# First stage of the second batch on sums and differences of x, two matmuls a piece in place of four

## The chip, the cores and the metric

One core of one Trainium2 chip runs the kernel. The metric is device time in microseconds, the median of several runs. TensorE is called PE here, with PEld for its weight loads, VectorE is DVE, ScalarE is ACT, GpSimd is POOL, SyncE is SP; SPq, ACTq and DVEq are their sequencers.

## The reference

For x of 8 batches, 3008 positions and 256 channels: a real FFT along the positions, a complex 256x256 projection with bias, a soft threshold at 0.01, the inverse FFT, and then a two-layer MLP on all 24064 tokens.

```python
X = np.fft.rfft(x, axis=1)
Yr = Xr @ w_r - Xi @ w_i + b_r
Yi = Xr @ w_i + Xi @ w_r + b_i
Yr = np.sign(Yr) * np.maximum(np.abs(Yr) - lam, 0.0)      # Yi likewise
y = np.fft.irfft(Yr + 1j * Yi, n=x.shape[1], axis=1)
h = y.reshape(B * S, D) @ w_in                            # 256 -> 2048
out = np.maximum(0.01 * h, h) @ w_out                     # 2048 -> 256
```

## The kernel before

The length 3008 is split as 47 x 64, and the transform is done as two stages of matmuls with constant matrices (`fa` for the factor 47, `fb` for 64), the projection between them and two inverse stages (`gb`, `ga`).

`fwd(b)` (L218) is the first stage of batch b. It loads x in seven pieces (L224, the DMA issues at L237 and L240), six of 120x512 and one, number 6, of 120x256. Each piece has two halves xa and xb (`xin`), on which the symmetry of the transform can be used: one half of the output is fa0 applied to the sum xa + xb, the other is fa1 applied to the difference xa − xb. In batch 0 and in batches 2 to 7 `fold` (L242) forms the sum and the difference on VectorE (L247, L248), and `stage_a` (L260) does one product of each. Batch 1 has its own function, `stage_a1` (L273), which works on xa and xb as loaded: fa0·xa + fa0·xb and fa1·xa + (−fa1)·xb, so four matmuls a piece, each of which shows as two records on PE. The negated matrix is the third slice of `fa32`, made by ACT in the set-up. ACT copies the two results over xa and xb (L282) and SP stores them to `u_dram` (L283). The pieces come in the order 0, 1, 2, 3, 6, 4, 5; 4 and 5 use the two banks `psf`, the others the four banks `psh`. The loads of batch 1 may not be issued before a certain read of batch 0 (`reads[-1]`), and its matmuls not before the last but one `stage_g` of batch 0 (`turning[NPAIR - 2]`).

`mid(b)` (L314) is the middle of batch b, in twelve pairs of frequencies: load u (L331), `stage_b` (L336, matmul L345, copy `ef` L349, sum L350), `proj` (L364, through `products`, whose matmuls are all at L80; bias sum `kb` L382, t L390, threshold c L391 and t L392, copies and signs `zf` L396 and L400), and `stage_g` (L412), which stores v to `v_dram` (L418, L420).

`v_load` (L455, DMA issue L461) and `inverse` (L470) turn one pair of columns back into tokens: matmuls with `ga` (L482), the copy `odd` (L485), sum and difference `y` (L486, L488), copies into `yc` (L495). `forms` (L498) makes of a chunk of 512 tokens the hi and lo parts that the MLP multiplies (`yh` L507, `yl` L508). The MLP (`moe_a`, `moe_b`, `moe_o`, the matmuls at L94 and L609) runs over 47 chunks.

`convert_win` (L159) and `load_wout` (L177) make hi and lo parts of the MLP's weights; most of that is on VectorE (L135 to L139, L164, L167 to L174, L203, L204). Two of its tiles, `cva` and `cvq`, take the buffers that are otherwise `vin`'s and `gf`'s.

Batch 0 is done first, ahead of the MLP. Three places are spoken of below. The batch-0 stage is the middle of batch 0, from about 42 to 100 us. The ramp, from 100 to about 120 us, holds the first five pieces of batch 1, the first two pairs of inverses and the end of the weight conversion. Behind it the MLP runs, and pieces 4 and 5 of batch 1 and the work of all later batches are mixed into it. A scheduler sets the order on each engine from the program and its own view of time; each engine takes its instructions in the order it is given, and waits by semaphores.

Of the kernel before, what the change touches and what calls it, by code (L numbers as in the profile page):

```python
# [8 lines left out]
F32 = mybir.dt.float32  # L9
# [11 lines left out]
P = 128  # L21
PA = NK1 * NG
# [8 lines left out]
def spectral_mlp_kernel(  # L31
# [18 lines left out]
    D = w_r.shape[0]  # L50
# [15 lines left out]
    sb = ctx.enter_context(tc.tile_pool(name="sb", bufs=2))  # L66
    dram = ctx.enter_context(tc.tile_pool(name="dram", bufs=2, space=bass.MemoryType.DRAM))
    ps = ctx.enter_context(tc.tile_pool(name="ps", bufs=1, space=bass.MemoryType.PSUM))
    sync, act, dve, pool = nc.sync, nc.scalar, nc.vector, nc.gpsimd

    def bank(tag, bufs):
        return ps.tile([P, 512], F32, name=tag, tag=tag, bufs=bufs)

    def products(dst, pairs):

        terms = []
        for l, r in pairs:
            terms += [(l[0], r[0]), (l[0], r[1]), (l[1], r[0])] if len(l) == 2 else [(l[0], r[0])]
        for i, (a, b) in enumerate(terms):
            last = nc.tensor.matmul(dst, a, b, start=(i == 0), stop=(i == len(terms) - 1))  # L80
        return last
# [14 lines left out]
    def flat(t):  # L96
        return t.rearrange("p a b -> p (a b)")


    consts = {}  # L100
# [117 lines left out]
    def fwd(b):  # L218
        ud = dram.tile([2, NK1, NG * NS, D], F32, name="u_dram", tag="u_dram", bufs=NPRE + 1)
        u_dram[b] = ud  # L220
        uv = ud.rearrange("c k (g s) d -> c (k g) (s d)", g=NG)
        x_t, s_t = {}, {}

        def load(c):  # L224
            cols = slice(2 * c * D, min(2 * c + 2, NS) * D)
            n = cols.stop - cols.start
            if b < NPRE:
                tag, bufs = (XT, XT1)[b][c]
                x2 = sb.tile([PA, 2, 2 * D], F32, name="xin", tag=tag, bufs=bufs)
                x_t[c] = [x2[:, h, :n] for h in range(2)]  # L230
            else:
                x_t[c] = [
                    sb.tile([PA, 2 * D], F32, name=f"xin{h}", tag="uv"[h], bufs=3 - h)[:, :n] for h in range(2)
                ]
            for h, t in enumerate(x_t[c]):
                if b == 0:
                    (act if h else sync).dma_start(t, x[b, h, :, cols])  # L237
                else:
                    with tc.issue_after(reads[-1].ins):
                        sync.dma_start(t, x[b, h, :, cols])  # L240

        def fold(c):  # L242
            xa, xb = x_t[c]
            n = xa.shape[1]
            eng = dve
            xs = sb.tile([PA, 2 * D], F32, name="xs", tag="zf", bufs=1)[:, :n] if b else xs3[:, c % 3, :n]
            eng.tensor_add(xs, xa, xb)  # L247
            eng.tensor_sub(xa, xa, xb)  # L248
            s_t[c] = [(xs,), (xa,)] if b < NPRE else [xs, xa]

        def split(c, h):
            t = s_t[c][h]
            n = t.shape[1]
            z = sb.tile([PA, 2, 2 * D], F32R, name="xz", tag="ez"[h], bufs=1)
            xh, xl = z[:, 0, :n], z[:, 1, :n]
            dve.tensor_copy(xh, t)
            dve.tensor_sub(xl, t, xh.bitcast(F32))  # L257
            s_t[c][h] = (xh, xl)

        def stage_a(c, h):  # L260
            t = x_t[c][h]
            n = t.shape[1]
            pa = (bank("psf", 2) if b else bank("psh", 4))[:PA, :n]
            products(pa, [(consts[f"fa{h}"] if b else consts[f"fa{h}32"], s_t[c][h])])
            t = x_t[c][1 - h]
            cp = act.copy(t, pa)
            if b == 0:
                turned[:] = [cp]
            st = (act if b else sync).dma_start(uv[h, :, 2 * c * D:2 * c * D + n], t)
            if b == 0:  # L270
                written.append(st)

        def stage_a1(c):  # L273

            n = x_t[c][0].shape[1]
            pas = [(bank("psf", 2) if c in (4, 5) else bank("psh", 4))[:PA, :n] for _ in range(2)]
            for h in range(2):
                with tc.issue_after(turning[NPAIR - 2].ins):
                    products(pas[h], [
                        (consts[f"fa{h}32"], (x_t[c][0],)), (consts[f"fa{2 * h}32"], (x_t[c][1],))])  # L280
            for h in range(2):
                act.copy(x_t[c][h], pas[h])  # L282
                sync.dma_start(uv[h, :, 2 * c * D:2 * c * D + n], x_t[c][h])  # L283

        if b == 1:
            for c in range(NX):
                load(c)
                yield 0
            for c in (0, 1, 2, 3, 6, 4, 5):
                stage_a1(c)  # L290
                yield 6 * x_t[c][0].shape[1]
            return

        ahead = 2 if b >= NPRE else NX
        for c in range(ahead):
            load(c)
        yield 4 * CS if b >= NPRE else 0
        fold(0)
        if b >= NPRE:
            split(0, 0)  # L300
        yield 0
        for c in range(NX):
            for h in range(2):
                if h == 0 and c + ahead < NX:
                    load(c + ahead)
                if h == 0 and c + 1 < NX:
                    fold(c + 1)
                stage_a(c, h)
                if b >= NPRE and (c + h < NX):
                    split(c + h, 1 - h)  # L310
                yield 3 * x_t[c][h].shape[1]


    def mid(b):  # L314
# [49 lines left out]
        def proj(j):  # L364

            e = e_t.pop(j)
            ps_k = bank("psf", 2) if b else bank("pso", 2)
            ps_y = None if b else bank("psf", 2)
            for dst, c, w in ((0, 2, "wr"), (0, 1, "wn"), (D, 0, "wd")):
                if c == 1 and b:  # L370
                    ps_y = bank("psf", 2)
                with tc.issue_after(mlp[0].ins) if b and c == 2 else nullcontext():
                    products((ps_k if c == 2 else ps_y)[:, dst:dst + D], [
                        (tuple(t[:, a, c, :] for t in e), tuple(t[:, a, :] for t in consts[w]) if b else (consts[w + "32"][0][:, a, :],)) for a in range(NH)
                    ])
                if c == 2:
                    kc = ps_k[:, :D]
                    if b:
                        kc = sb.tile([P, D], F32, name="kc", tag="kc")
                        act.copy(kc, ps_k[:, :D])  # L380
                    kb = sb.tile([P, 2, D], F32, name="kb", tag="kb", bufs=1)
                    (pool if b else dve).tensor_add(kb, bias, kc.unsqueeze(1).broadcast_to([P, 2, D]))  # L382
                if c:
                    yield 6 * D
                if c == 2 and b and j:
                    stage_g(j - 1)
                    yield 3 * CS
            t = sb.tile([P, 2, D], F32, name="t", tag="t" if b else "v", bufs=1 if b else 2)
            c = sb.tile([P, 2, D], F32, name="c", tag="kb" if b else "yt", bufs=1)
            dve.tensor_add(flat(t), ps_y, flat(kb))  # L390
            dve.tensor_scalar(c, t, LAMBDA, -LAMBDA, ALU.min, ALU.max)  # L391
            thresholded.append(dve.tensor_sub(t, t, c))  # L392
            zf = z0[j % 3] if b == 0 else sb.tile([P, 2, D], F32, name="zf", tag="zf", bufs=1)
            for i in range(2):
                s = slice(64 * i, 64 * (i + 1))
                act.copy(zf[:64, i, :], t[s, 0, :])  # L396
                if b == 0 and j == NPAIR - 1:
                    dve.tensor_scalar(zf[64:, i, :], t[s, 1, :], sign[s, NK1 + j:NK1 + j + 1], None, ALU.mult)
                else:
                    act.mul(zf[64:, i, :], t[s, 1, :], sign[s, NK1 + j:NK1 + j + 1])  # L400
            if b == 0:
                z_t[j] = (zf,)
                yield 6 * D
                return
            z = sb.tile([P, 2, 2, D], F32R, name="zh", tag="z", bufs=1)
            zh, zl = z[:, 0], z[:, 1]
            act.copy(zh, zf)
            dve.tensor_sub(zl, zf, zh.bitcast(F32))
            z_t[j] = (zh, zl)
            yield 6 * D  # L410
# [273 lines left out]
    FWD = NS * 6 * D  # L684


    fa32 = sb.tile([PA, 3, PA], F32, name="fa32", tag="xi", bufs=1)
    for h in range(2):
        sync.dma_start(fa32[:, h], fa[h])
    for h in range(3):  # L690
        consts[f"fa{h}32"] = (fa32[:, h],)
    xs3 = sb.tile([PA, 3, 2 * D], F32, name="xs3", tag="yl")
    f0 = Stream(fwd(0), FWD)
# [10 lines left out]
    win_tmp = (  # L704
        sb.tile([P, NH * NIN], F32, name="cva", tag="vin"), sb.tile([P, NH * NIN], F32, name="cvq", tag="gf"),
        sb.tile([P, 4, 2, P], F32, name="ws", tag="yh"))
    act.mul(fa32[:, 2], fa32[:, 1], -1.0)
    convert_win(0)
    with tc.issue_after(turned[0].ins):
        split_consts()  # L710
# [162 lines left out]
```

## Time and profile before

| | us |
|---|---|
| median of 3 runs | 2574.14 |
| lowest and highest | 2566.14, 2575.76 |
| the profiled execution | 2568.88 |
| its span on the core | 2567.1 |

The mean granted clock of PE in the profiled execution is 0.995 of full speed. The rows below are of that one execution: busy times by engine, stretches of time with the busy time of each engine, single instructions with their start and duration, and what ended a wait. A count behind an x is a number of instructions that stand together on one engine.

### The profile page before, as it was taken

How to read it: one execution, taken by the hardware profiler on the slowest of the kernel's cores; microseconds unless marked ns; L12 is line 12 of the kernel's file. 1: busy time of each engine (PE TensorE's matmuls, PEld its weight loads, DVE VectorE, ACT ScalarE, POOL GpSimd, SP SyncE). 2: the span in 40 equal slices, each digit the busy share in tenths (PEclk: the TensorE clock that was granted, in tenths of full speed). 3: DMA queues.
4: the chain of work that ended last, by engine and by line, in shares of the span. 5: the costliest groups of instructions: out<-in, count | busy, mean ns of one | idle time of the engine just before them, and what ended most of it. 6: DMA issues, size and time to landing. Idle time of an engine off the chain costs nothing.

```text
span 2567.1 us, 42449 instructions
## 1 busy us (share of the span) xinstructions
PE 2527.2 (98%) x16204; PEld 2269.8 (88%) x16204; DVE 1882.8 (73%) x3460; ACT 1677.5 (65%) x3151; POOL 118.9 (5%) x96
## 2 busy tenths in 40 slices
PE   6999999999999999999999999999999999999999
PEld 4689888999899998999989999899998998999998
DVE  7787777777877778777787677867768777666665
ACT  4776666677566765677666676567665676655564
POOL 0001000000000000000000000000000000000000
PEclk8999999999999999999999999999999999999999
DMA  8631133111321113111141111412114111100000
GB/s 267 176 93 50 42 91 88 41 50 45 103 67 46 50 37 112 59 49 49 42 113 53 50 49 38 120 54 58 34 38 132 46 54 41 44 21 29 9 17 17
DMA packets 119904, 165.12 MB, mean 64 GB/s; under 512 B 13597, under 2 KB 69909, under 8 KB 119701
## 3 DMA queue, kind: packets, MB, share of 16 engines
q1 hardware_dynamic: 79112, 115.54, 14.7%
q10 hardware_dynamic: 40589, 46.87, 7.1%
q8 instruction: 128, 2.10, 0.4%
q14 instruction: 75, 0.61, 0.1%
HBM read 86.60 MB, written 75.76 MB: 63 GB/s over the span
## 4 chain that ended last, share of the span: by engine, by line
PE 89%; DMA 4%; DVE 3%; ACT 2%; issue 1%; ACTq 0%; SPq 0%; DVEq 0%
PE pso L609 38%; PE psh L94 34%; PE psf L80 11%; PE psf L482 3%; PE psf L345 3%; DMA xin<-x_dram 1%; DMA u_dram<-xin 1%; PE psh L80 1%; DVE gl L562 1%; DMA v_dram<-v 0%; DMA u<-u_dram 0%; DVE xz L257 0%; DVE gf L593 0%; ACT zf L400 0%; DMA vin<-v_dram 0%
## 5 line engine op out<-in xcount | busy, mean ns | idle before, releaser
L94 PE MATMUL psh<-yh,win_hi 128*128 128x256 f32 (+1 forms) x2608 | 741.3, 285 | 2.1 <-DVE gf L593 2.0
L94 PE MATMUL psh<-yl,win_hi 128*128 128x256 f32 (+1 forms) x2608 | 732.3, 281 | 0.0
L94 PE MATMUL psh<-yh,win_lo 128*128 128x256 f32 (+1 forms) x2608 | 729.6, 281 | 0.0
L562 DVE TENSOR_TENSOR gl<-gf,gh 128x1024 fp32r<-128x1024 f32 x376 | 461.0, 1226 | 309.8 <-ACT gh L560 305.9
L609 PE MATMUL pso<-gl,wout_hi 128*128 128x512 f32 x1504 | 591.6, 393 | 1.1 <-DVE gl L562 1.1
L609 PE MATMUL pso<-gh,wout_hi 128*128 128x512 f32 x1504 | 591.1, 393 | 1.0 <-ACT gh L560 1.0
L609 PE MATMUL pso<-gh,wout_lo 128*128 128x512 f32 x1504 | 589.6, 392 | 0.0
L94 PEld LDWEIGHTS psh<-yh,win_hi 128*128 128x128 f32 x2608 | 489.9, 188 | 19.7 <-DVE gf L593 4.9
L94 PEld LDWEIGHTS psh<-yl,win_hi 128*128 128x128 f32 x2608 | 490.4, 188 | 17.4 <-issue 0.5
L94 PEld LDWEIGHTS psh<-yh,win_lo 128*128 128x128 f32 x2608 | 489.0, 188 | 2.1
L560 ACT CAST gh<-gf 128x1024 fp32r<-128x1024 f32 x376 | 395.3, 1051 | 44.4 <-PE pso L609 34.9
L596 ACT ACTIVATE gf<-gf 128x768 f32<-128x768 f32 x368 | 311.7, 847 | 150.4 <-DVE gf L593 139.4
L609 PEld LDWEIGHTS pso<-gl,wout_hi 128*128 128x128 f32 x1504 | 282.5, 188 | 61.4 <-DVE gl L562 2.9
L609 PEld LDWEIGHTS pso<-gh,wout_hi 128*128 128x128 f32 x1504 | 282.8, 188 | 47.3 <-ACT gh L560 1.8
L609 PEld LDWEIGHTS pso<-gh,wout_lo 128*128 128x128 f32 x1504 | 282.5, 188 | 46.5 <-issue 0.2
L595 ACT ACTIVATE gf<-psh 128x256 f32<-128x256 f32 x368 | 142.0, 386 | 239.1 <-PE psh L94 232.0
L593 DVE TENSOR_TENSOR gf<-psh,u 128x512 f32<-128x512 f32 x368 | 252.4, 686 | 34.4 <-PE psh L94 30.7
L577 ACT COPY p<-psh 128x256 f32<-128x256 f32 x368 | 137.0, 372 | 158.0 <-PE psh L94 149.6
L382 POOL TENSOR_TENSOR kb<-bias,kc 128x512 f32<-128x512 f32 x84 | 116.3, 1385 | 2074.3 <-ACT kc L380 1877.0
L578 DVE TENSOR_TENSOR u<-psh,p 128x256 f32<-128x256 f32 x368 | 154.6, 420 | 73.8 <-ACT p L577 72.6
L580 DVE TENSOR_TENSOR gf<-psh,u 128x256 f32<-128x256 f32 x368 | 154.8, 421 | 31.1 <-PE psh L94 17.2
L581 DVE TENSOR_TENSOR gf<-psh,gf 128x256 f32<-128x256 f32 x368 | 154.5, 420 | 5.5
(128 smaller groups left out, 3173.0 us busy)
## 6 DMA issues: line engine op xcount, KB each, us to landing
u<-u_dram SPq DMA_DIRECT2D x192, 128.0 KB, 2.8
v_dram<-v ACTq DMA_DIRECT2D x192, 128.0 KB, 2.4
out_dram<-ob SPq DMA_DIRECT2D x94, 256.0 KB, 2.0
vin<-v_dram SPq DMA_DIRECT2D x96, 240.0 KB, 3.6
xin<-x_dram SPq DMA_DIRECT2D x90, 240.0 KB, 3.0
u_dram<-xin ACTq DMA_DIRECT2D x72, 240.0 KB, 2.4
u_dram<-xin SPq DMA_DIRECT2D x24, 240.0 KB, 4.4
raw<-w_out_dram SPq DMA_DIRECT2D x8, 512.0 KB, 5.3
```

Of the source, the lines that this page charges most:

```text
L80: last = nc.tensor.matmul(dst, a, b, start=(i == 0), stop=(i == len(terms) - 1))
L94: mlp[:] = [nc.tensor.matmul(dst, a, b, start=start and i == 0, stop=i == 2, skip_group_check=True)]
L560: cp = act.copy(gh, g)
L562: parted[:] = [cp, dve.tensor_sub(gl, g, gh.bitcast(F32))]
L577: act.copy(p1, b1[:, lo])
L578: dve.tensor_add(u2, b1[:, hi], p1)
L580: dve.tensor_add(g[:, 3], b2[:, hi], u2)
L581: dve.tensor_add(g[:, 3], b2[:, lo], g[:, 3])
L593: dve.tensor_add(g[:, 1:3], b2.rearrange("p (k n) -> p k n", k=2), u2.unsqueeze(1).broadcast_to([P, 2, HT]))
L595: act.activation(g[:, 0], b1[:, lo], AF.Prelu, alpha=SLOPE)
L596: act.activation(g[:, 1:4], g[:, 1:4], AF.Prelu, alpha=SLOPE)
L609: mlp[:] = [nc.tensor.matmul(po, a[:, f, s], r[:, i], start=(f == 0 and j == 0), stop=(f == NF - 1 and j == 2),)]
```

## The change

For each piece of batch 1 VectorE forms xs = xa + xb in a new tile and then xa − xb in place of xa; fa0 is multiplied with xs and fa1 with the difference, two matmuls in place of four. The new tile `xs` takes two buffers under the tag "t", which before had one and belonged to the tile t of `proj` in batches 1 to 7; that tile now has two as well. The third slice of `fa32` and its negation on ACT are gone. Behind the changed lines the new program's line numbers are 3 higher, down to the set-up.

```diff
@@ stage_a1
             pas = [(bank("psf", 2) if c in (4, 5) else bank("psh", 4))[:PA, :n] for _ in range(2)]
+            xs = sb.tile([PA, 2 * D], F32, name="xs", tag="t", bufs=2)[:, :n]
+            xa, xb = x_t[c]
+            dve.tensor_add(xs, xa, xb)
+            dve.tensor_sub(xa, xa, xb)
             for h in range(2):
                 with tc.issue_after(turning[NPAIR - 2].ins):
-                    products(pas[h], [
-                        (consts[f"fa{h}32"], (x_t[c][0],)), (consts[f"fa{2 * h}32"], (x_t[c][1],))])
+                    products(pas[h], [(consts[f"fa{h}32"], ((xs, xa)[h],))])
@@ proj
-            t = sb.tile([P, 2, D], F32, name="t", tag="t" if b else "v", bufs=1 if b else 2)
+            t = sb.tile([P, 2, D], F32, name="t", tag="t" if b else "v", bufs=2)
@@ set-up
-    fa32 = sb.tile([PA, 3, PA], F32, name="fa32", tag="xi", bufs=1)
+    fa32 = sb.tile([PA, 2, PA], F32, name="fa32", tag="xi", bufs=1)
     for h in range(2):
         sync.dma_start(fa32[:, h], fa[h])
-    for h in range(3):
         consts[f"fa{h}32"] = (fa32[:, h],)
@@ weights
-    act.mul(fa32[:, 2], fa32[:, 1], -1.0)
```

VectorE's order in the batch-0 stage before, where batch 0's t, c and `ef` are mixed with the weight conversion:

```order
L350 TENSOR_TENSOR ef_230<-ef_230 128x2x128
L391 TENSOR_SCALAR c_374<-t_373 128x512
L137 SCALAR_TENSOR_TENSOR cva_180<-win_raw_252,cva_180 128x1024
L392 TENSOR_TENSOR t_373<-t_373,c_374 128x512
L350 TENSOR_TENSOR ef_230<-ef_230 128x2x128
L138 TENSOR_SCALAR win_raw_252<-cva_180 128x1024
L139 TENSOR_TENSOR cvq_181<-cvq_181,win_raw_252 128x1024
L382 TENSOR_TENSOR kb_402<-bias_249,pso_398 128x512
```

The same place in the new order (xs_744 and xin_423 are piece 0, xs_755 is piece 1):

```order
L279 TENSOR_TENSOR xs_744<-xin_423 120x512
L394 TENSOR_SCALAR c_373<-t_372 128x512
L137 SCALAR_TENSOR_TENSOR cva_180<-win_raw_251,cva_180 128x1024
L280 TENSOR_TENSOR xin_423<-xin_423 120x512
L395 TENSOR_TENSOR t_372<-t_372,c_373 128x512
L353 TENSOR_TENSOR ef_229<-ef_229 128x2x128
L138 TENSOR_SCALAR win_raw_251<-cva_180 128x1024
L385 TENSOR_TENSOR kb_401<-bias_248,pso_397 128x512
L139 TENSOR_TENSOR cvq_181<-cvq_181,win_raw_251 128x1024
L393 TENSOR_TENSOR t_407<-psf_398,kb_401 128x512
L279 TENSOR_TENSOR xs_755<-xin_444 120x512
```

The sum of piece 0 stands right ahead of batch 0's c, and the difference and piece 1's sum follow among the steps of batch 0.

VectorE's order in the ramp before, at the end of the conversion of `w_in` (`ws`, `cva`, `win_lo`):

```order
L169 TENSOR_TENSOR ws<-ws,cva 128x256
L174 TENSOR_TENSOR win_lo<-cva,win_hi 128x2x256
L174 TENSOR_TENSOR win_lo<-cva,win_hi 128x256
L138 TENSOR_SCALAR raw<-cva 128x512
L170 TENSOR_TENSOR ws<-cva,ws 128x256
L139 TENSOR_TENSOR cvq<-cvq,raw 128x512
L203 TENSOR_TENSOR cva<-cva,wout_hi 128x512
```

The same place in the new order; the adds of pieces 2, 3 and 6 stand ahead of these rows:

```order
L138 TENSOR_SCALAR raw<-cva 128x512
L174 TENSOR_TENSOR win_lo<-cva,win_hi 128x256
L169 TENSOR_TENSOR ws<-ws,cva 128x256
L139 TENSOR_TENSOR cvq<-cvq,raw 128x512
L203 TENSOR_TENSOR cva<-cva,wout_hi 128x512
L489 TENSOR_TENSOR y<-psf,odd 128x240
L491 TENSOR_TENSOR y<-psf,odd 128x230
L170 TENSOR_TENSOR ws<-cva,ws 128x256
```

L170 now stands behind L139, L203 and the two y operations of the first inverse.

SP's order in the ramp before, where the loads of `vin` for the first two pairs of inverses and the stores of batch 1's pieces are mixed:

```order
L461 DMA vin<-v_dram 120x512
L283 DMA u_dram<-xin 120x512
L461 DMA vin<-v_dram 120x512
L283 DMA u_dram<-xin 120x512 x3
L461 DMA vin<-v_dram 120x512 x2
L188 DMA raw<-w_out_dram 128x2x512 x2
L283 DMA u_dram<-xin 120x512 x4
L283 DMA u_dram<-xin 120x256 x2
```

And in the new order:

```order
L464 DMA vin<-v_dram 120x512
L286 DMA u_dram<-xin 120x512 x4
L464 DMA vin<-v_dram 120x512
L286 DMA u_dram<-xin 120x512 x4
L286 DMA u_dram<-xin 120x256 x2
L464 DMA vin<-v_dram 120x512 x2
L188 DMA raw<-w_out_dram 128x2x512 x2
```

The second load of the first pair moved behind four stores, the two loads of the second pair behind all ten.

## The prediction

> **What bounds the kernel now.** The page first: which engine is busy, and what ends the chain.
>
> ```profile
> span 2567.1 us, 42449 instructions
> PE 2527.2 (98%) x16204; PEld 2269.8 (88%) x16204; DVE 1882.8 (73%) x3460; ACT 1677.5 (65%) x3151; POOL 118.9 (5%) x96
> PE 89%; DMA 4%; DVE 3%; ACT 2%; issue 1%; ACTq 0%; SPq 0%; DVEq 0%
> ```
>
> PE is busy for 2527.2 of 2567.1 us, so 39.9 us of idle time are all that anything but PE's own work can give, and cutting PE's work looks like the only lever. But the work cut here lies in the first 150 us, where the kernel is not yet in its steady state. So the busy time by stretches comes next (columns: stretch, sum, PE, PEld, DVE, ACT, POOL, granted clock, DMA share, GB/s).
>
> ```profile
> 60.00:70.00 10.00, 7.49 (x34) 5.47 (x34) 7.88 (x17) 5.83 (x11) 0.00 (x0) 1.00 0.78 218
> 80.00:90.00 10.00, 9.77 (x48) 7.52 (x47) 4.25 (x8) 6.97 (x15) 0.00 (x0) 1.00 0.27 69
> 100.00:110.00 10.00, 10.00 (x25) 4.22 (x24) 9.90 (x18) 6.08 (x11) 0.00 (x0) 1.00 0.70 195
> 110.00:120.00 10.00, 9.55 (x49) 6.69 (x48) 6.92 (x14) 6.27 (x14) 0.00 (x0) 1.00 0.94 297
> 120.00:130.00 10.00, 10.00 (x40) 6.79 (x40) 8.18 (x15) 8.48 (x17) 0.00 (x0) 1.00 0.40 106
> ```
>
> From 100 to 110 us VectorE is 99% busy beside a full PE: it converts weights there. That is where the first adds of the change are wanted. Up to 95 us runs the middle of batch 0 (the batch-0 stage), from 100 to 119 us the ramp, behind it the MLP.
>
> **PE's work: two matmuls for four.** The timeline of PE (start, duration, engine, line, count) has the whole first stage of batch 1.
>
> ```profile
> 100.54 10.46 PE L80 MATMUL psh<-xin,fa 120*120 120x512 f32 x24
> 111.74 4.46 PE L80 MATMUL psh<-xin,fa 120*120 120x512 f32 x12
> 116.70 1.03 PE L80 MATMUL psh<-xin,fa 120*120 120x256 f32 x4
> 120.17 0.72 PE L94 MATMUL psh<-yh,win_hi 128*128 128x512 f32 x2
> ```
>
> The rest of it stands in the chain of waits (start, duration, engine, tile, line, count):
>
> ```profile
> 121.83 3.43 PE psf L80 x8
> 137.30 1.72 PE psf L80 x4
> 143.16 1.72 PE psf L80 x4
> ```
>
> Five pieces stand in the ramp: 10.46 + 4.46 + 1.03 = 15.95 us, of which half, 8.0 us, goes. Pieces 4 and 5 stand inside the MLP (the chain's rows): 3.43 + 1.72 + 1.72 = 6.87 us, half of it 3.4 us. All that PE can save is 11.4 us, 0.44% of the span. A measurement of this kernel tells about 0.5%, 12.9 us, from no change.
>
> The 3.4 us lie between MLP blocks that follow each other without a gap and count in full: **−3.4** (bounds −3.4 and 0, the latter if their adds are late). The adds for them stand between weight conversions with a slack of several microseconds. The 8.0 us of the ramp count only if what PE does next is ready that much sooner: the inverses (L482) and the first MLP block at 120.17. That is worked out below.
>
> **VectorE's adds.** The adds of batch 0's fold are the same instructions (grouped by form: ns at least, median, most).
>
> ```profile
> L247 DVE TENSOR_TENSOR xs<-xin x7: 418/693/694, 6.1 to 17.4; 120x512 f32<-120x512 f32 x6, 120x256 f32<-120x256 f32 x1
> ```
>
> Twelve adds at 0.693 us and two at 0.418: 9.1 us on VectorE. In the order the adds of pieces 0 and 1 stand in the batch-0 stage, those of 2, 3 and 6 in the ramp, those of 4 and 5 in the MLP.
>
> **The batch-0 stage.** The first add stands between `ef` (L350) and `c` (L391), and needs both halves of x's piece 0. On VectorE's queue `c`, and with it the chain t, zf, matmul of batch 0, stand behind that wait. The rows are of SP's DMA issues and of their time to land, of VectorE and of ACT.
>
> ```profile
> 52.27 1.05 SPq L240 DMA_DIRECT2D xin<-x_dram  x2
> xin<-x_dram SPq DMA_DIRECT2D x2, 240.0 KB, 5.0
> 58.74 0.35 SPq L240 DMA_DIRECT2D xin<-x_dram  x1
> 54.39 0.42 DVE L350 TENSOR_TENSOR ef<-ef 128x256 f32<-128x256 f32 x1
> 54.72 0.42 DVE L391 TENSOR_SCALAR c<-t 128x512 f32<-128x512 f32 x1
> 63.27 0.68 DVE L392 TENSOR_TENSOR t<-t,c 128x512 f32<-128x512 f32 x1
> 66.91 0.41 ACT L396 COPY zf<-t 64x256 f32<-64x256 f32 x1
> ```
>
> The two loads are issued between 52.27 and 53.32 and take 5.0 us at the median, so the second lands by about 58.3; SP, which waits for such a load, goes on at 58.74. VectorE would start `c` at 54.72; it waits to 58.7 instead: 4.0 us. Four adds follow in the same stretch, 4 × 0.693 = 2.8 us. Together VectorE is 6.8 us behind at `t` (L392, done at 63.27 + 0.68 = 63.95). ACT takes it at 66.91, a slack of 3.0, so ACT gets it 3.8 late. From 70 us on PE has no idle time in which to catch up (60–70: 7.49 busy, 80–90: 9.77), while VectorE has. So the lag stays on PE. Bounds: 0 (the loads come early and the queue's other steps hide it) and 6.8 (no slack holds); I take **+4.5**, nearer to 3.8, which the one slack that the trace shows gives, than to 6.8.
>
> **The ramp.** Two things hold the inverses now. In SP's order the second load of `vin` for the first pair stands behind four stores of u, and the two for the second pair behind all ten of the ramp instead of four. And the second pair's `vin` shares its buffer with `cva`, so its loads wait for the conversion's L170.
>
> ```profile
> 104.48 0.32 SPq L461 DMA_DIRECT2D vin<-v_dram  x1
> 105.36 0.34 SPq L461 DMA_DIRECT2D vin<-v_dram  x1
> 108.04 0.42 DVE L170 TENSOR_TENSOR ws<-cva,ws 128x256 f32<-128x256 f32 x1
> 108.58 1.21 SPq L461 DMA_DIRECT2D vin<-v_dram  x2
> DMA to landing us min/median/max: 3.0/4.3/4.9
> 118.04 0.36 ACT L485 COPY odd<-psf 128x240 f32<-128x240 f32 x1
> ```
>
> Today L170 ends at 108.46 and the loads go out at 108.58. In the new order four adds of 0.693 and two of 0.418 (3.6 us) stand ahead of it, then L139 and L203, moved ahead (1.4), then the two `y` operations (0.8): 108.0 + 5.8 = 113.8. VectorE was 99% busy, so nothing hides this. The loads go out near 114.0, land 3.0 to 4.9 later (116.9 to 118.8), 16 inverse records at about 0.13 (1.05 for 8 at 148.86, quoted below) take 2.1, and the `odd` copy starts near 119.7 (119.2 to 121.1) in place of 118.04. From there to the first MLP block the steps are the same. So the MLP starts 1.6 us later, not 8.0 sooner: **+1.6**, bounds −1.0 (the `y` steps and the stores come early) and +3.1. PE, relieved of 8.0 us, stands idle for some 6 us here.
>
> **The clock.** PE's gaps now grow by 3.8 us in the batch-0 stage and to 6 us in the ramp. What a gap does:
>
> ```profile
> 360.00:365.00 5.00, 2.96 (x16) 1.71 (x14) 4.90 (x11) 1.45 (x3) 0.00 (x0) 1.00 0.73 202
> 365.00:370.00 5.00, 4.85 (x17) 3.65 (x18) 3.83 (x8) 2.34 (x6) 0.00 (x0) 0.66 0.58 162
> 35.47 5.46 PE L345 MATMUL psh<-fb,u 128*128 128x128 f32 x24 [9.06 <-DMA u<-u_dram]
> 40.00:42.00 2.00, 2.00 (x11) 1.87 (x10) 1.97 (x4) 0.00 (x0) 0.00 (x0) 0.80 0.90 279
> ```
>
> At 360 us PE idles for 2.04 us, and in the next 5 us the clock is 0.66: 1.7 us of work lost. After the long gap before 35.47 the clock is 0.80 over 40–42, so full from about 40.8: 5.3 us at half, 2.7 lost. In 60–70, with 2.51 us idle in parts, it stayed at 1.00. So either gap may cost 1.7 to 2.7 or nothing; I take one of the two, at the lower price, that of the gap nearer in length: **+1.7**, bounds 0 and 5.4. The Trainium skill, "TensorE: Matmul & The Clock Gate", section "Part 1: The HAM clock gate", says that the clock is halved after at least one idle window of about 3.4 us and comes back after about 3.4 us of sustained work. By that rule both gaps would pay, 3.4 us in all in place of 1.7, and the forecast would be 1.7 us higher; the row at 365 agrees with the return (34% missing of 5 us, at half clock 3.4 us), while that at 360 shows a gap in the sum of only 2.04 us before it.
>
> **Chunk 1.** In PE's order the last inverse ahead of chunk 1 of the MLP stands later among the blocks.
>
> ```profile
> 148.86 1.05 PE L482 MATMUL psf<-ga,vin 120*128 120x128 f32 x8
> 155.20 0.69 DVE L508 TENSOR_TENSOR yl<-yc,yh 128x512 fp32r<-128x512 f32 x1
> 158.74 0.69 DVE L508 TENSOR_TENSOR yl<-yc,yh 128x512 fp32r<-128x512 f32 x1
> 155.44 2.79 PE psh L94 x12
> ```
>
> From the inverse to the first `yl` pass 155.89 − 148.86 = 7.0 us, to a later one 10.6. Behind the inverse the new order leaves about two and a half blocks of 12 at 2.79 us, 6.9, before chunk 1. So 0.1 to 3.7 us, and 0 if they stay ahead; **+0.5**.
>
> The dropped negation on ACT, the smaller `fa32` and the second `t` buffer of the later batches cost or bring nothing: they lie at the start, beside loads, or bind nobody. The steady state behind 170 us keeps its work.
>
> Sum: 4.5 + 1.6 + 1.7 + 0.5 − 3.4 = **+4.9 us**. The profiled execution took 2568.88 us (span 2567.1 and 1.8 around it), so it would be 2573.8; it was 5.3 below the median of the runs (2574.14, from 2566.14 to 2575.76). By the median: **2579.0 us**. Its own range, from the bounds that matter most (0 to 6.8 in the stage, −1.0 to 3.1 in the ramp, 0 to 5.4 for the clock), is 2571 to 2588.
>
> **Rivals.** (1) *The batch-0 stage isn't delayed*: the load lands before VectorE gets there, or the 3.0 us of slack and the idle time in 60–70 take all. For it: PE idles 2.5 us in 60–70 already. Against: the load was issued only 2.4 us before VectorE reaches that place. Then 1.6 + 0.5 − 3.4 with at most one clock drop: −1.3 to +0.4, about 2573.5. (2) *PE's saving arrives in full*: the ramp is bound by PE, as 10.00 of 10 in 100–110 suggests, and the inverses move up with it. Against: `vin` waits for VectorE at 9.90 of 10. −11.4: 2562.7. (3) *Slower, the clock falls and stays down in the batch-0 stage*: work and gaps alternate there, as from 20 to 41 us.
>
> ```profile
> 20.00:22.00 2.00, 1.07 (x2) 0.54 (x3) 1.50 (x3) 2.00 (x5) 0.00 (x0) 0.58 1.08 347
> ```
>
> The clock was 0.58 there, and still 0.80 at 40 to 42. At half clock for 20 us, 10 us of work are lost: 4.9 − 1.7 + 10 = +13.2, 2587.3. The point from which it decides: a clock under 0.6 for 15 us or more between 55 and 100. Against: 1.00 in 60–70 in spite of short gaps. The change surely does what it says: half of the matmuls are gone from the order.
>
> **Chances.** Forecast 0.62, rival (1) 0.21, (2) 0.06, (3) 0.11. The range of 8 in 10 goes from 2566 to 2588: it reaches over rival (1) with the runs' own spread (their lowest is 8 below the median), leaves out rival (2) and the upper half of (3). Faster by over 0.5% (under 2561.3) needs more than PE's whole saving: only rival (2) with a low run, 0.03. Slower by over 0.5% (over 2587.0): half of (3) and the forecast's upper end, 0.09. Within 0.5%: 0.88.
>
> **What would show it.** Right: VectorE idle for about 4 us before the first `xs`, ended by the x load; ACT's `zf` some 4 us later; L170 near 114 plus that delay; a gap of PE of about 6 us ended by `vin`; the first L94 near 128 in place of 120.17. Wrong in the stage: `zf` on time. Wrong in the ramp: PE's gap ended by anything but `vin`, or none over 3 us. Wrong in the clock: 1.00 throughout, or under 0.7 for long. If the time falls by 8 us or more, the view that VectorE and the buffer of `vin` bound the ramp is wrong.

## The result and the profile after

The changed kernel takes 2598.65 us (2595.28 to 2603.7) against 2572.43 us (2566.14 to 2575.76) of the kernel before in the same runs: ratio 1.0114, 95% interval 1.0101 to 1.0127, so about 26 us slower. The forecast was 2579.0, in a range up to 2588.

The page of the changed kernel: span, busy time, the chain by engine, and the three costliest groups (count, busy us, mean ns, idle before).

```profile
span 2596.5 us, 42413 instructions
PE 2544.2 (98%) x16176; PEld 2289.5 (88%) x16176; DVE 1890.6 (73%) x3474; ACT 1678.6 (65%) x3150; POOL 118.6 (5%) x96
PE 94%; DMA 2%; DVE 1%; ACT 1%; SPq 0%; issue 0%; ACTq 0%; DVEq 0%
L94 PE MATMUL psh<-yh,win_hi 128*128 128x256 f32 (+1 forms) x2608 | 746.5, 287 | 2.6 <-ACT yh L510 1.7
L94 PE MATMUL psh<-yl,win_hi 128*128 128x256 f32 (+1 forms) x2608 | 739.9, 284 | 0.3 <-DVE yl L511 0.2
L94 PE MATMUL psh<-yh,win_lo 128*128 128x256 f32 (+1 forms) x2608 | 739.7, 285 | 0.0
```

The same groups of the kernel before:

```profile
L94 PE MATMUL psh<-yh,win_hi 128*128 128x256 f32 (+1 forms) x2608 | 741.3, 285 | 2.1 <-DVE gf L593 2.0
L94 PE MATMUL psh<-yl,win_hi 128*128 128x256 f32 (+1 forms) x2608 | 732.3, 281 | 0.0
L94 PE MATMUL psh<-yh,win_lo 128*128 128x256 f32 (+1 forms) x2608 | 729.6, 281 | 0.0
```

PE has fewer matmuls than before and is busy for 17 us longer: the MLP's own matmuls, which the change doesn't touch, take 22.9 us more in these three rows. That is the first sign that the larger part of the loss has nothing to do with batch 1's first stage. The second sign is when the time is lost. The MLP has 12336 matmuls, the same in every kernel; the table gives how much later than in the trace of the kernel before the first, the 201st, the 1201st and the last of them start (us; there at 120.2, 173.0, 397.4 and 2562.7), for the changed kernel and all that follow.

| kernel | 1st | 201st | 1201st | last | median us | ratio to before (95%) |
|---|---|---|---|---|---|---|
| changed | 9.9 | 11.0 | 13.1 | 29.5 | 2598.65 | 1.0101 to 1.0127 |
| a_pad | 12.6 | 13.7 | 15.9 | 17.8 | 2585.77 | 1.004 to 1.007 |
| a_64 | 11.6 | 12.7 | 12.9 | 12.5 | 2581.43 | 1.0035 to 1.0062 |
| b_shift32 | −0.6 | −0.9 | 1.4 | −1.1 | 2566.67 | 0.9974 to 0.9993 |
| b_shift64 | 0.5 | 0.8 | 2.1 | 20.6 | 2589.4 | 1.0058 to 1.0091 |
| b_shift128 | 2.0 | 2.0 | 2.8 | 10.8 | 2578.19 | 1.0022 to 1.0046 |
| b_shift160 | 0.5 | 0.7 | 0.4 | −1.9 | 2567.86 | 0.9979 to 0.9997 |
| b_all64 | 1.7 | 1.7 | 3.5 | 2.4 | 2567.9 | 0.9983 to 1.0001 |
| b_win64 | 3.1 | 3.4 | 6.5 | 24.6 | 2590.55 | 1.0069 to 1.0096 |
| b_yl64 | 1.4 | 1.4 | 1.3 | 6.0 | 2575.61 | 1.0014 to 1.0032 |
| b_wout64 | 4.8 | 5.0 | 7.9 | 27.1 | 2589.07 | 1.0057 to 1.0088 |
| a_pad_pool | 5.9 | 3.4 | 11.5 | 12.5 | 2581.65 | 1.0027 to 1.0057 |
| b_inplace | 5.8 | 4.3 | 11.8 | 10.9 | 2578.01 | 1.002 to 1.0045 |
| b_half | 1.3 | −0.8 | 5.8 | 4.7 | 2574.33 | 1.0012 to 1.0031 |
| a_fill | 9.0 | 11.6 | 13.6 | 12.3 | 2584.41 | 1.0043 to 1.007 |
| b_45 | 0.2 | 1.0 | 3.4 | 2.8 | 2572.04 | 1.0 to 1.0017 |

In the changed kernel some 10 us are lost before the MLP starts, and 16.4 us between its 1201st and its last matmul, spread over the whole of that stretch. Lags of one execution have a spread of their own: b_win64 and b_wout64, whose order is that of the kernel before, start the MLP 3.1 and 4.8 us late, b_shift32 0.6 early. The last column but one, over several runs, carries the verdicts.

The start first. The busy time by stretches of the changed kernel:

```profile
70.00:80.00 10.00, 7.70 (x31) 5.74 (x32) 8.15 (x17) 7.21 (x14) 0.00 (x0) 0.83 0.47 127
100.00:110.00 10.00, 6.39 (x9) 2.42 (x9) 7.28 (x13) 4.94 (x10) 0.00 (x0) 0.69 0.46 99
110.00:120.00 10.00, 8.00 (x25) 3.63 (x23) 9.98 (x21) 6.78 (x15) 0.00 (x0) 0.97 0.82 253
120.00:130.00 10.00, 4.56 (x23) 4.33 (x24) 6.71 (x13) 4.09 (x8) 0.00 (x0) 0.66 0.76 226
130.00:140.00 10.00, 8.11 (x29) 5.77 (x29) 7.95 (x15) 7.93 (x17) 0.00 (x0) 0.83 0.21 58
```

PE, which was full here, is busy for 4.56 of 10 us at 120, and the clock is below 1.00 in all five stretches: 1.7 + 3.1 + 0.3 + 3.4 + 1.7 = 10.2 us of clock gone. The instructions that the forecast spoke of, in order of time:

```profile
58.62 0.69 DVE L279 TENSOR_TENSOR xs<-xin 120x512 f32<-120x512 f32 x1 [3.03 <-DMA xin<-x_dram]
72.31 3.00 PE L80 MATMUL psf<-w,ef 128*128 128x256 f32 x8 [2.31 <-DVE t L393]
108.81 0.69 DVE L279 TENSOR_TENSOR xs<-xin 120x512 f32<-120x512 f32 x1 [2.40 <-PE psh L80]
114.70 5.53 SPq L286 DMA_DIRECT2D u_dram<-xin  x6
119.66 0.42 DVE L170 TENSOR_TENSOR ws<-cva,ws 128x256 f32<-128x256 f32 x1
120.33 0.84 SPq L464 DMA_DIRECT2D vin<-v_dram  x2
124.10 3.74 PE L485 MATMUL psf<-ga,vin 120*128 120x128 f32 x16 [5.07 <-DMA vin<-v_dram]
127.93 0.36 ACT L488 COPY odd<-psf 128x240 f32<-128x240 f32 x1 [3.15 <-PE psf L485]
130.07 0.71 PE L94 MATMUL psh<-yh,win_hi 128*128 128x512 f32 x2
```

VectorE waits for x until 58.62, and PE then waits 2.31 us for VectorE's t. In the ramp VectorE waits 2.40 us for a matmul of batch 1: `xs` has two buffers, and this is the third sum. L170 ends at 120.1, and the last of the ten stores of u has been issued by 120.2. The second pair's `vin` stands behind both; it goes out at 120.33, and PE waits 5.07 us for it.

### The profile page after: what moved, and what is told of

Its sections match the earlier page's. It is cut to its first block, busy times and chain, and to the rows that moved or that the text cites. A ratio compares the mean times of both kernels' runs of the same rounds, so it can differ in the third digit from the quotient of the medians.

```text
span 2596.5 us, 42413 instructions
## 1 busy us (share of the span) xinstructions
PE 2544.2 (98%) x16176; PEld 2289.5 (88%) x16176; DVE 1890.6 (73%) x3474; ACT 1678.6 (65%) x3150; POOL 118.6 (5%) x96
## 4 chain that ended last, share of the span: by engine, by line
PE 94%; DMA 2%; DVE 1%; ACT 1%; SPq 0%; issue 0%; ACTq 0%; DVEq 0%
PE pso L612 39%; PE psh L94 36%; PE psf L80 11%; PE psf L485 3%; PE psf L348 3%; DMA xin<-x_dram 1%; PE psh L80 1%; DMA u<-u_dram 0%; DMA u_dram<-xin 0%; DMA vin<-v_dram 0%; DVE gl L565 0%; ACTq L423 0%; DMA win_raw<-w_in_dram 0%; ACT zf L403 0%; ACT zf L399 0%
## 5 line engine op out<-in xcount | busy, mean ns | idle before, releaser
L94 PE MATMUL psh<-yh,win_hi 128*128 128x256 f32 (+1 forms) x2608 | 746.5, 287 | 2.6 <-ACT yh L510 1.7
L94 PE MATMUL psh<-yl,win_hi 128*128 128x256 f32 (+1 forms) x2608 | 739.9, 284 | 0.3 <-DVE yl L511 0.2
L94 PE MATMUL psh<-yh,win_lo 128*128 128x256 f32 (+1 forms) x2608 | 739.7, 285 | 0.0
L612 PE MATMUL pso<-gl,wout_hi 128*128 128x512 f32 x1504 | 591.6, 393 | 1.5 <-DVE gl L565 1.5
L94 PEld LDWEIGHTS psh<-yh,win_hi 128*128 128x128 f32 x2608 | 491.9, 189 | 19.3 <-DVE gf L596 2.4
L94 PEld LDWEIGHTS psh<-yl,win_hi 128*128 128x128 f32 x2608 | 492.3, 189 | 18.3 <-DVE yl L511 1.2
L94 PEld LDWEIGHTS psh<-yh,win_lo 128*128 128x128 f32 x2608 | 490.8, 189 | 2.1
```

The source lines that it names most:

```text
L94: mlp[:] = [nc.tensor.matmul(dst, a, b, start=start and i == 0, stop=i == 2, skip_group_check=True)]
L612: mlp[:] = [nc.tensor.matmul(po, a[:, f, s], r[:, i], start=(f == 0 and j == 0), stop=(f == NF - 1 and j == 2),)]
```

## The experiments

### Addresses: the part of the loss in the MLP

With two slices in place of three, the place that `fa32` shares with the later tile `xi` shrinks from 1440 to 1024 bytes a partition, and every tile behind it in SBUF, up to those of the last few kilobytes, stands 416 bytes lower. In the program as built, yh goes from byte 158528 to 158112 and yl from 84800 to 84384, while the weights win stay at 7712 and 36384.

**a_pad**, the change with the third slice kept, unused:

```diff
-    fa32 = sb.tile([PA, 2, PA], F32, name="fa32", tag="xi", bufs=1)
+    fa32 = sb.tile([PA, 3, PA], F32, name="fa32", tag="xi", bufs=1)
```

> The changed kernel with fa32 kept at three slices, the third unused; the order on every engine is that of the changed kernel. In the changed kernel the smaller fa32 moved every tile behind it by 416 bytes a partition: yh from byte 158528 (a multiple of 64) to 158112 (32 past one), yl from 84800 to 84384. Theory A (addresses): the lag behind the kernel before, which grows from 11 us at 196 us to 29.5 us at the end, comes from these addresses; then the steady state goes back to a start-to-start time of 117 ns for the 256-wide L94 matmuls, the lag stays near 11 us, and the time is 2572 + 9 to 11 = 2581 to 2584. Theory B (the work: second t buffer, another order of the later batches): nothing changes, 2598. Theory C (the lag belongs to the chip that the profile was taken on): the time is 2598 and the lag of this profile is as it falls.

Measured: 2585.77 us, 12.9 below the changed kernel. The lag grows by 1.9 us from the 1201st matmul to the last, in place of 16.4, and the MLP's groups are back:

```profile
L94 PE MATMUL psh<-yh,win_hi 128*128 128x256 f32 (+1 forms) x2608 | 740.8, 285 | 4.3 <-DVE gf L596 2.6
L94 PE MATMUL psh<-yl,win_hi 128*128 128x256 f32 (+1 forms) x2608 | 733.4, 282 | 0.3 <-DVE yl L511 0.2
L94 PE MATMUL psh<-yh,win_lo 128*128 128x256 f32 (+1 forms) x2608 | 730.1, 281 | 0.0
```

Theories B and C fall. The time itself lies 2 us above what A gave, since the start was 2 to 3 us worse than in the profile of the change.

**b_shift32**, **b_shift64**, the kernel before with all tiles behind `fa32` 32 or 64 bytes further (8 or 16 floats):

```diff
-    fa32 = sb.tile([PA, 3, PA], F32, ...)
+    fa32 = sb.tile([PA, 3 * PA + 8], F32, ...)[:, :3 * PA].rearrange("p (h k) -> p h k", h=3)
```

> The kernel before with fa32 eight floats wider, so that all tiles behind it stand 32 bytes further; the order on every engine is that of before. Theory A (addresses): the start is as before and the lag grows by 0.78 us in 100 us from the start of the MLP on, 18 to 19 us in all: 2590 to 2592. Theories B and C: 2572, no lag.

> The kernel before with fa32 sixteen floats wider, all tiles behind it 64 bytes further; the order is that of before. Theory A in the form that only a place within 64 bytes counts: 2572, as before. In the form that a place within 128 bytes counts (yh stood 64 past a multiple of 128 before, and now on one): another time, a gain of up to 20 us if the half step of 32 bytes cost 18. Theories B and C: 2572.

Both expectations missed: 32 bytes cost nothing (2566.67), while 64 bytes, for which theory A had no loss in either form, cost 18 us (2589.4). The same group in both:

```profile
L94 PE MATMUL psh<-yh,win_lo 128*128 128x256 f32 (+1 forms) x2608 | 729.1, 281 | 0.0
```

```profile
L94 PE MATMUL psh<-yh,win_lo 128*128 128x256 f32 (+1 forms) x2608 | 735.9, 283 | 0.0
```

So addresses alone, with the order of before on every engine, make a loss of this size; but it isn't a matter of multiples of 64 bytes.

**a_64**, the change with its two slices and 64 bytes behind them:

```diff
-    fa32 = sb.tile([PA, 2, PA], F32, ...)
+    fa32 = sb.tile([PA, 272], F32, ...)[:, :2 * PA].rearrange("p (h k) -> p h k", h=2)
```

> The changed kernel with two slices of fa32 as it is, and 64 bytes behind them, so that yh stands at byte 158176 of a partition (96 past a multiple of 128; changed kernel 32, kernel before 64). In the runs so far the offset of yh, yl and the MLP's tiles from a multiple of 128 bytes was 64 and 96 in the fast ones (before, 32 bytes further) and 0 and 32 in the slow ones (64 bytes further, the changed kernel). Theory A, a period of 128 bytes: the lag no longer grows in the MLP, and the time is that of the changed kernel with its addresses restored, 2582 to 2589. Rival, the extent of the shift or the dropped slice itself counts: 2598.

Measured 2581.43, no growth in the MLP (12.9 to 12.5): the dropped slice itself costs nothing.

**b_all64** adds 64 bytes ahead of win, so that weights and moving tiles shift together; **b_win64** shifts win by 64 and the others by 128:

```diff
-    sign = const.tile([P, NK1 + NPAIR], F32, name="sign")
+    sign = const.tile([P, NK1 + NPAIR + 16], F32, name="sign")[:, :NK1 + NPAIR]
```

(b_win64 has the `fa32` line of b_shift64 as well.)

> The kernel before with 64 bytes added ahead of the MLP's weights win, so that win and all tiles that were moved by 64 bytes in the slow run are moved together: win at 96 past a multiple of 128 (was 32), yh at 0 (was 64). Theory A1 (what counts is where the MLP's moving tile stands against the weights that are loaded beside it): as before, 2571. Theory A2 (the place of yh and its like by itself counts): slow, 2589.

> The kernel before with win moved by 64 bytes (96 past a multiple of 128) and the other tiles by 128 (yh at 64, as before). Theory A1 (place against the weights): slow, 2589, with the lag growing over the MLP. Theory A2 (place of yh by itself): as before, 2571.

Measured 2567.9 and 2590.55. The group in b_all64 and in b_win64:

```profile
L94 PE MATMUL psh<-yh,win_lo 128*128 128x256 f32 (+1 forms) x2608 | 729.6, 281 | 0.0
```

```profile
L94 PE MATMUL psh<-yh,win_lo 128*128 128x256 f32 (+1 forms) x2608 | 735.2, 283 | 0.0
```

In b_all64, yh stands at the byte that was slow in b_shift64, and the group is that of before to the tenth of a microsecond. In b_win64, yh stands where it was modulo 128, and it is slow. A2 falls: what counts is where tiles stand against each other, not where yh stands by itself. Both runs are as A1 has it.

**b_wout64**, the second weights 64 bytes further (128 bytes added to each, the view begun 16 floats in; in the program as built wout_hi moves by 64 bytes, wout_lo by 192 and yh by 128, while win, yl, gh and gl stay):

```diff
-            sb.tile([P, NF, D], F32R, ...)
+            sb.tile([P, NF * D + 32], F32R, ...)[:, 16:16 + NF * D].rearrange(...)
```

> The kernel before with the MLP's second weights (wout, loaded beside the moving gh and gl) 64 bytes further, all else at the same place modulo 128 bytes; the order is that of before. In the kernel before gh, gl and wout stand at the same offset (64), which for yh and win (offset difference 0) was a slow case. If the same rule holds for L609: its start-to-start falls from 227 by 2 to 10 ns, 4512 matmuls, 9 to 45 us: 2525 to 2562. If the rule doesn't reach 512-wide matmuls (a weight load takes less than half of each): 2571, start-to-start 227 as before.

Both expectations missed: 2589.07. The group with wout_lo has 595.4 us in place of 589.6 before, and L94's with win_lo 734.2, though win did not move and yh moved by 128:

```profile
L94 PE MATMUL psh<-yh,win_lo 128*128 128x256 f32 (+1 forms) x2608 | 734.2, 283 | 0.0
...
L609 PE MATMUL pso<-gh,wout_lo 128*128 128x512 f32 x1504 | 595.4, 396 | 0.0
```

So the place matters for L609 too, but it became slower where the rule had it faster, and for L94 the period isn't 128 bytes. One row doesn't fit A1 either: the group of yl with win_hi takes 736.3 us in place of 732.3, though neither yl nor win moved. Three more runs were made on the period.

**b_yl64** moves yl by 64 bytes against win (yh, gh, gl and wout by 1024), **b_shift128** and **b_shift160** all tiles behind `fa32` (32 and 40 floats in place of 8):

```diff
-        yh, yl = y_t[ci] = tuple(sb.tile([P, 7, HT], F32R, name=n_, tag=n_) for n_ in ("yh", "yl"))
+        yh = sb.tile([P, 7, HT], F32R, name="yh", tag="yh")
+        yl = sb.tile([P, 7 * HT + 128], F32R, ...)[:, 16:16 + 7 * HT].rearrange("p (k n) -> p k n", k=7)
+        y_t[ci] = (yh, yl)
```

> The kernel before with yl alone 64 bytes further against the weights win, all other tiles at the same place modulo 512 bytes; the order is that of before. Theory A1, moving tile against the weights loaded beside it: only the matmuls with yl (2608 of the 7824 at L94) become slower, by 2 to 2.5 ns: 5 to 7 us, 2574 to 2577. Rival, a common cause outside these operands: all three kinds of L94 matmul slower or none, 2587 or 2569.

> The kernel before with all tiles behind fa32 128 bytes further. Period of 128 bytes: as before, 2569, L94 start-to-start 117.3 ns. By the mean over the runs so far at that difference within 512 bytes (118.4 at 416, where yh stood with wout moved): 7 to 10 us more, 2576 to 2580.

> The kernel before with all tiles behind fa32 160 bytes further. Period of 128 bytes: as with 32 bytes, 2565 to 2568. By the mean at that difference within 512 bytes (116.7 ns for L94 in the run with the changed kernel and 64 bytes, against 117.3 before): 4 to 6 us less from L94, some of it lost again at L609: 2564 to 2568. Both give much the same; slower than 2569 would speak against both.

The times are 2575.61, 2578.19 and 2567.86. b_shift128 lies in the range that goes by the place within 512 bytes, and refutes a period of 128 bytes; b_shift160 lies in its ranges too, but these were much the same and decide nothing. The time of b_yl64 is the one that A1 gave, but its rows are not: A1 had only the matmuls of yl slower. These take 735.9 us in place of 732.3, and those of yh with win_lo, which follow them, 735.2 in place of 729.6.

```profile
L94 PE MATMUL psh<-yh,win_hi 128*128 128x256 f32 (+1 forms) x2608 | 743.4, 286 | 2.4 <-DVE gf L595 2.4
L94 PE MATMUL psh<-yl,win_hi 128*128 128x256 f32 (+1 forms) x2608 | 735.9, 283 | 0.0
L94 PE MATMUL psh<-yh,win_lo 128*128 128x256 f32 (+1 forms) x2608 | 735.2, 283 | 0.0
```

L609 doesn't go by A1 alone either: in b_shift160 gl and wout_hi move together, and still the group of the two takes 588.8 us in place of 591.6. Which tiles have to stand where, and with what period, stays open; that two reads get in each other's way is a guess that no run here tests.

### The start: adds, matmuls and gaps

**a_pad_pool**, a_pad with the adds on GpSimd:

```diff
-            dve.tensor_add(xs, xa, xb)
-            dve.tensor_sub(xa, xa, xb)
+            pool.tensor_add(xs, xa, xb)
+            pool.tensor_sub(xa, xa, xb)
```

> The changed kernel with fa32 at three slices and the sums and differences on GpSimd in place of VectorE; VectorE's order is that of before. If the waits on VectorE (the first add on its x load, 4 us; the adds ahead of L170, 3.6 us) and the clock that falls in the gaps behind them are the cause of the first 10 us of lag: the batch-0 stage ends at 100 us as before, the second pair's vin is issued near 108.6, and the MLP starts at or before 120, the time 2572 - 3.4 (pieces 4 and 5) to 2572 - 11.4: 2561 to 2569. If PE's halved work itself leaves gaps in which the clock falls, or the order of SP's stores holds vin: the MLP starts at 120 or later and the time is 2569 to 2580.

The batch-0 stage ends as before: its last matmul of `zf` starts at 100.24 (before 100.11, changed kernel 106.01, a_pad 109.04). So the delay of the stage is the adds on VectorE. But the ramp isn't freed (VectorE and GpSimd, then PE's wait and the first MLP block):

```profile
102.34 2.17 DVE L139 TENSOR_TENSOR cvq<-cvq,win_raw 128x1024 f32<-128x1024 f32 x1
...
110.94 3.12 POOL L279 TENSOR_TENSOR xs<-xin 120x512 f32<-120x512 f32 x2
...
114.26 3.15 DVE L174 TENSOR_TENSOR win_lo<-cva,win_hi 128x512 fp32r<-128x512 f32 x2
...
121.24 5.11 PE L485 MATMUL psf<-ga,vin 120*128 120x128 f32 x24 [8.65 <-DMA vin<-v_dram]
126.11 0.72 PE L94 MATMUL psh<-yh,win_hi 128*128 128x512 f32 x2
```

VectorE has the same instructions in the same order here as before, without idle time, but they take longer while GpSimd adds: L139 2.17 us in place of 1.23, the two L174 3.15 in place of 1.02, and so on. From this L139 to L170 pass 15.3 us in place of 5.8; L170 starts at 117.67, and the second pair's `vin` loads wait for it. Time 2581.65: the second case of the expectation, and 1.7 us beyond it, but for a reason that it didn't have.

```profile
102.21 1.23 DVE L139 TENSOR_TENSOR cvq<-cvq,win_raw 128x1024 f32<-128x1024 f32 x1
106.77 1.02 DVE L174 TENSOR_TENSOR win_lo<-cva,win_hi 128x512 fp32r<-128x512 f32 x2
```

(Those two rows are the kernel before.)

**b_inplace**, the kernel before with sum and difference formed in place, the five pieces of the ramp at 80 to 97 us:

```diff
+            xa, xb = x_t[c]
+            with tc.issue_after(thresholded[7 if c < 2 else 8].ins):
+                dve.tensor_add(xa, xa, xb)
+                dve.scalar_tensor_tensor(xb, xb, -2.0, xa, ALU.mult, ALU.add)
...
+                    products(pas[h], [(consts[f"fa{h}32"], (x_t[c][h],))])
```

> The kernel before with two matmuls a piece, but the sum formed in xa and the difference in xb as xa minus twice xb, so that no new tile is needed, addresses as before, and the adds of the five pieces of the ramp placed behind batch 0's t of pairs 7 and 8 (80 to 97 us), where VectorE was 43% busy. If the cost at the start is the adds' place on VectorE (4 us of wait in the batch-0 stage, 3.6 us ahead of L170): the stage ends at 100 to 102 us, L170 near 108, the second pair's vin goes out near 109 and lands by 113, the MLP starts at 116 to 119, and with pieces 4 and 5 the time is 3 to 8 us under before: 2563 to 2568. Rival, the gap that PE's halved work leaves costs as much through the clock and through vin behind the stores: 2569 to 2576.

Measured 2578.01, above the first case and 2 us above the rival's end. The adds ran at 85 to 94 us and the stage ended at 103.50. (Some of that may be the spread of single executions: b_wout64, with the order of before, has 103.48; the changed kernel, a_64 and a_pad have 106.01, 108.45 and 109.04.) L170 came at 111.22, but the second pair's loads went out later still, behind stores of u, and the MLP starts at 125.96:

```profile
114.34 0.63 SPq L464 DMA_DIRECT2D vin<-v_dram  x1
115.89 0.42 SPq L464 DMA_DIRECT2D vin<-v_dram  x1
```

With the adds out of the ramp the halved matmuls still bring nothing. The next run takes the adds out altogether.

**b_half**, the kernel before without the second half's products:

```diff
-                    products(pas[h], [
-                        (consts[f"fa{h}32"], (x_t[c][0],)), (consts[f"fa{2 * h}32"], (x_t[c][1],))])
+                    products(pas[h], [(consts[f"fa{h}32"], (x_t[c][0],))])
```

> The kernel before with the products of x's second half left out (two matmuls a piece on xa alone, no adds; batch 1's first stage is not computed in full). VectorE has no more to do than before, PE as little as in the change, addresses as before. If the adds on VectorE alone cost the time at the start: stage at 100 us, L170 near 108, the MLP starts at 114 to 117, pieces 4 and 5 bring 3.4 us: 2559 to 2566. If PE's matmuls in the ramp only filled a chain that is as long without them (v store, vin load, inverse, y, yh): the MLP starts at 118 to 123, with half clock behind PE's gap, and the time is 2566 to 2575.

Measured 2574.33, ratio 1.0021 (1.0012 to 1.0031): less work on PE, no adds, and not faster. The MLP starts at 121.46, in the second case's band. PE waits for `vin` and then works at a lower clock (SP's two loads for the second pair first):

```profile
110.03 1.05 SPq L460 DMA_DIRECT2D vin<-v_dram  x1
112.12 0.42 SPq L460 DMA_DIRECT2D vin<-v_dram  x1
...
111.70 0.71 PE L481 MATMUL psf<-ga,vin 120*128 120x128 f32 x4 [2.45 <-DMA vin<-v_dram]
114.67 3.75 PE L481 MATMUL psf<-ga,vin 120*128 120x128 f32 x16 [2.26 <-DMA vin<-v_dram]
...
121.46 1.20 PE L94 MATMUL psh<-yh,win_hi 128*128 128x512 f32 x2
```

```profile
110.00:120.00 10.00, 4.70 (x21) 4.28 (x22) 5.39 (x11) 3.35 (x9) 0.00 (x0) 0.70 0.94 327
```

So PE's 8 us in the ramp filled a chain of stores, loads, inverse and forms that comes out as long without them. L170 is on time here (108.18), but the two loads stand behind seven and eight stores of u and go out at 110.03 and 112.12, before from 108.58 on. No run restores SP's order alone, so it stays open how much of the chain's length is that order and how much the lower clock.

**a_fill**, a_pad with each product issued twice:

```diff
+                    for _ in range(2):
-                    products(pas[h], [(consts[f"fa{h}32"], ((xs, xa)[h],))])
+                        products(pas[h], [(consts[f"fa{h}32"], ((xs, xa)[h],))])
```

> The changed kernel with the addresses restored and each of the two products of a piece issued twice, so that PE has the work of before and VectorE that of the change. Theory gaps (the loss in the ramp comes from PE's gaps and the half clock behind them): few windows of half clock behind 100 us, the MLP starts 4 to 7 us later than before (the batch-0 stage's delay), time 2575 to 2580. Theory adds (VectorE's adds delay the chain whatever PE does): MLP start 10 to 13 us later as with two matmuls, time 2581 to 2589.

Measured 2584.41, as a_pad within the intervals: the theory of the adds by its time. The MLP starts 9.0 us late, between the two bands. From the stage's last `zf` matmul to the first L94 pass 24.1 us (105.13 to 129.18), as in the change (106.01 to 130.07) and not 20.1 as before. Full work on PE doesn't help: with the adds on VectorE the ramp is this long with half of PE's work and with all of it.

**b_45**, two matmuls for pieces 4 and 5 alone, in the way of b_inplace:

```diff
+            if c in (4, 5):
+                dve.tensor_add(xa, xa, xb)
+                dve.scalar_tensor_tensor(xb, xb, -2.0, xa, ALU.mult, ALU.add)
```

> The kernel before with two matmuls in place of four for pieces 4 and 5 alone, which lie inside the MLP, the sum in xa and the difference in xb, addresses as before. If PE's saving counts where it lies in a stretch without gaps: 3.4 us off, 2565 to 2568, the start as before up to 120 us. If the reordering or the wait ahead of chunk 1 takes it: 2569 to 2573.

Measured 2572.04, ratio 1.0 to 1.0017: the 3.4 us don't arrive.

```profile
123.72 0.50 PE L94 MATMUL psh<-yh,win_hi 128*128 128x512 f32 x1 [1.68 <-ACT yh L511]
```

```profile
120.00:130.00 10.00, 8.10 (x30) 5.78 (x30) 8.21 (x15) 8.19 (x16) 0.00 (x0) 0.83 0.44 112
```

PE now waits 1.68 us for chunk 0's second part of yh. Before, piece 4's matmuls stood there and covered it; in the new order they stand from 138.54 on. The clock falls to 0.83 in that stretch, 1.7 us, and the saving is gone in place. The changed kernel has the same wait, 1.66 us at 133.38, with piece 4 from 148.78 on.

Part of the loss of a_pad_pool, b_inplace and b_half comes later, between the 201st and the 1201st matmul (6.6 to 8.1 us). PE waits there 4.8 to 5.4 us for VectorE's `xz` (L256, of the later batches' first stage) in place of 1.8 before, and 2.8 us for ACT's `ob`, and from 140 to 410 us 5.1 to 6.8 us of clock are missing in place of 1.7. Their order is another there; no run isolates it. No kernel here beats the kernel before by more than 0.2%; the nearest, b_shift32 and b_shift160, leave batch 1 alone.

## Why the prediction was wrong

- **The step that failed** is the sentence that "the smaller `fa32` and the second `t` buffer of the later batches cost or bring nothing", with "the steady state behind 170 us keeps its work". The work stayed, but its speed did not. Moving the tiles cost 12.9 us by the medians of the changed kernel and a_pad, 17.2 by those of the changed kernel and a_64, and 16.4 in the traces. That is 16.4 us / 11136 = 1.5 ns on average for each MLP matmul from the 1201st on. With the old addresses (a_pad) the time lies inside the stated range.
- **The batch-0 stage** (+4.5) went as forecast: the first add waits until 58.62 (58.7 forecast), and ACT's `zf` starts at 70.65 in place of 66.91, 3.7 us late (3.8 forecast). The stage ends 5.9 us late, with 1.7 us of clock at 70 to 80 in it. a_pad_pool shows the cause.
- **The ramp** (+1.6): L170 was put at 113.8 with the stage on time, 119.7 with its 5.9 us; it starts at 119.66, and `vin` goes out at 120.33. That this fits so closely is luck in part: VectorE was only 4.2 us late at the last step ahead of the ramp's adds (L138, 105.72 in place of 101.48), and then waited 2.40 us for a buffer of `xs`, a wait that the prediction didn't have. Its `odd` at 119.7 goes with a landing of 3.6 us; with the median that it quotes, 4.3, it would be 120.4. The 16 inverse records took 3.74 us in place of 2.1 at the lower clock, and the ramp became 4.0 us longer. PE's saving of 8.0 us was rightly held for worthless in this order (b_half).
- **The clock** (+1.7, bounds 0 and 5.4) was mis-sized: 10.2 us of clock were missing between 70 and 140, a part of it in waits. The Trainium skill, "TensorE: Matmul & The Clock Gate", section "Part 1: The HAM clock gate", asks for about 3.4 us of idle; here the clock fell at 73 us behind a longest gap of 2.31 us, and the measurement decides. The 3.4 us that the prediction had by that rule were nearer than the value taken and still too low.
- **Pieces 4 and 5** (−3.4): their saving did not come, for a wait of 1.68 us and the clock behind it (b_45). The prediction had it count in full because PE showed no gap there; but piece 4 was what kept a gap from showing.
- **Chunk 1** (+0.5) cost nothing that the trace shows: PE is busy for 10.00 of 10 us in each stretch from 140 to 170.
- **The rivals**: (3) gave the nearest time, 2587.3, but not the cause: the clock was 0.83 and 1.00 over 70 to 90 us, not under 0.6 for 15 us. (1) and (2) fell. The bounds that the prediction names for its own range add up to 2570.2 and 2586.5 by the median, not quite the 2571 to 2588 that it gives.

Open: which tiles have to stand where, what SP's order costs by itself, and how the clock's loss splits between gaps that waited anyway and work.

## What to carry to other kernels

When a change alters a tile's size, compare the addresses of the tiles behind it before the new work is costed; a variant with the old addresses, or the old kernel with the new ones, separates the two in one run. A busy engine may only be filling the time of a chain that is as long without it: ask for each saved matmul what is ready at that moment, and what the gap does to the clock. A full VectorE makes an in-order add cost what queues behind it, not its own 0.69 us. A new tile with two buffers makes its third writer wait for the first reader, here 2.40 us: count the buffers when the wait is worked out.

## What the runs showed of the hardware

The rate of back-to-back 256-wide float32r matmuls depends on where the tiles stand against each other in SBUF: 64 bytes on all tiles behind `fa32`, yh and yl among them, with the same instructions in the same order, made 18 us in 2570 (b_shift64), and moving the weights along took it back (b_all64). The Trainium skill, "SBUF — State Buffer", section "SBUF: two separate sides", says that PE never waits on anyone; no run here shows whom it could wait for, but its pace depends on addresses all the same, so the measurement decides. The same section has VectorE and GpSimd share a port; in a_pad_pool the two L174 that took 3.15 us in place of 1.02 beside GpSimd's adds agree.
